# Another order of the first steps in a fused mLSTM and feed-forward kernel

## The chip, the cores and the metric

The kernel runs on one core of a Trainium2 chip. The metric is the device time of one execution in microseconds (us), as the median of several runs. Of TensorE (PE in the profile, PEld for its weight loads), VectorE (DVE), ScalarE (ACT), GpSimd (POOL) and SyncE (SP), the last one here only issues transfers.

## The reference

An mLSTM cell runs over 768 steps for 4 batches of 8 heads with 40 numbers each. Its output, as 3072 rows of 320 numbers, goes through a multiplicative feed-forward network.

```python
for t in range(S):
    m_new = np.maximum(f_gate[:, :, t] + m, i_gate[:, :, t])
    f_stab = np.exp(f_gate[:, :, t] + m - m_new)
    i_stab = np.exp(i_gate[:, :, t] - m_new)
    m = m_new
    C = f_stab[:, :, None, None] * C + i_stab[:, :, None, None] * np.einsum('bhd,bhe->bhde', vt, kt)
    n = f_stab[:, :, None] * n + i_stab[:, :, None] * kt
    h_tilde = np.einsum('bhde,bhe->bhd', C, qt)
    nq = np.einsum('bhd,bhd->bh', n, qt)[:, :, None]
    denom = np.maximum(np.abs(nq), 1.0)
    o = 1.0 / (1.0 + np.exp(-o_gate[:, :, t]))
    y[:, :, t] = o * h_tilde / denom
...
a = x @ w1          # x: (3072, 320), w1 and w2: (320, 1024)
b = x @ w2
h = a * b @ w3      # (1024, 1024)
return (h @ w_out)  # (1024, 320)
```

All data are float32. The weights come as 64-bit numbers, two 32-bit words each, and the kernel turns them into float32 on the chip.

## The kernel before, in words

**Units.** The sequence is cut into chunks of 128 steps (two halves of 64). A unit is one chunk of one batch with all 8 heads: 24 units, numbered from 0, the four batches of chunk 0 first. For a unit, PE transposes k and q (`turn`, tiles `pt`, copied to `kT` and `qT` by ACT), makes the scores inside each half (`cell<-qT,kT`) and the two updates of the state (`cell<-vw,kbuf`). POOL makes the weighted values `vw` (`weighted`, line 326). Decay weights `pw` come from a DVE transpose of a small table (`rows_of_u`, L291), an exponential on ACT (`weights`, L299, eight pieces) and a triangular mask on POOL (`masks`, L304). DVE multiplies scores by them (L388). In the next step PE makes the unit's output from these products (`ph` for units 0 and 1, `cell<-vbuf,pw` later) and from the state (`cell<-state,qT`); DVE scales and sums it (L412 to L419), forms the denominator (L427 to L430), and multiplies by the output gate (L432, L434) to `y`. `out_gate` is the tanh for it on ACT (L266). The state is updated by a DVE copy or addition (L397, L395), a POOL multiplication (`decayed`, L331) and a DVE addition (L403).

**Steps.** The loop over `s` handles unit s's scores and unit s−1's output in `quarter_work`. From step 2 on it also holds feed-forward work. A block is 128x512 products of w1 (`pa`) and of w2 (`pb`) for 256 rows; `up` does 256 of the 320 rows of the contraction, `up_rest` the remaining 64 against the tile `wr`. ACT then copies `pa` (`a_sb`, L624) and DVE multiplies it with `pb` (L625). Steps 2 to 5 have one block each, all on the rows of units 0 and 1; steps 2 and 3 use the first half of the weights' columns, steps 4 and 5 the second half. `x_trans` (tiles `px`, `xT`) turns a unit's `y` into the feed-forward input; `twice` (POOL, L465) doubles 64 of its columns first. `warm` issues fill matmuls.

**Words.** `fetch` (L180) loads a set of weight words. `scale_next` takes the next set through two ACT operations (L187, L191); for the first two sets DVE does the second (L189). `convert` makes float32 of it in two DVE operations (L195, L196). The sets of the first half are w1 twice, w2 twice and `wr`; the same five follow for the second half, then others.

**Order.** All transfers except the input gate and the output are issued from SP in program order. The order on each engine is that of the program, with a few operations held behind a named one (`issue_after`, `keep_order`); PE's order is chained by hand (`in_order`). So the change, which moves calls, moves instructions. Four PSUM buffers (`mps`) go round among the transposes and blocks: an operation that takes one waits until the reader of the fourth before it is done.

In step 2 the function `between` runs after unit 1's output and before unit 2's scores: it holds `x_trans` of units 0 and 1, conversions, the turn of unit 2 and the first block.

Of the kernel before, what the change touches and what calls it, by code (L numbers as in the profile page):

```python
# [16 lines left out]
def kernel(  # L17
# [211 lines left out]
    def scale_next(early=False):  # L229
        scaled.append(pend.pop(0))  # L230
        scale(scaled[-1][1], early)
# [101 lines left out]

    def quarter_work(s, rest, between):

# [53 lines left out]
        with tc.issue_after(first_read.ins) if first_read else nullcontext():  # L389
            if den:  # L390
                den()
            if n < NU:

                if c:
                    nc.vector.tensor_tensor(out=second, in0=pc[:, 0], in1=second, op=OP.add)  # L395
                else:
                    nc.vector.tensor_copy(out=second, in_=pc[:, 0])  # L397
                if len(ends) > 1:
                    decayed(after, second, n, 1)
            if den:  # L400
                den()
            if n < NU and len(ends) > 1:
                nc.vector.tensor_tensor(out=after, in0=pc[:, 1], in1=after, op=OP.add)  # L403
            if den:
                done = den()
        return done if den else first_read

    def outputs(n, pi, ph):
# [181 lines left out]
    for x in range(2):  # L590
        mm(pd[halves[x]], odd[:, x].to_broadcast([RG, L]), pick.rearrange("p j g c -> p (j g c)"))
    cols_of_u()
    nc.scalar.copy(out=decay.rearrange("p j c -> p (j c)"), in_=pd)
    rows_of_u(1)
    nc.scalar.activation(out=g, in_=U, func=AF.Exp)
    scale_next(True)
    convert()
# [142 lines left out]
    todo = w12[5:] + [("wo", i, 0) for i in range(FO)] + [("w3", ko, part) for ko in range(FO) for part in range(2)]  # L740
    n_cvt = [0, 0, 2, 0, 1, 2, 3, 3, 3] + [2] * 6
    n_fetch = [5, 5, 10]
    pinned, ahead = 32, 9
# [3 lines left out]
    for s in range(len(n_up)):  # L747
# [4 lines left out]
        if s < 3:  # L752
            if s == 2:
                for _ in range(3):
                    fetch(*todo.pop(0))
            load(s + 2, slice(0, 2))
            if s == 1:
                load_o(2)
            if s == 2:
                for _ in range(2):  # L760
                    fetch(*todo.pop(0))
                fetched = 10
            load(s + 2, slice(2, 3))
            if s:
                load_o(s + 2)
        elif s + 2 < NU:
            load(s + 2)
            load_o(s + 2)
# [26 lines left out]
        open_ups = [up(*x) for x in now] if s != 2 else []  # L795
        if s == 3:
            turn(3)
        def rest():
            for x in open_ups:
                up_rest(*x)  # L800
            if seven:
                seven[2]()
            if s == 3:
                for _ in range(2):
                    convert()

        def between():
            twice(1)
            weighted(2)
            rows_of_u(3)  # L810
            for _ in range(3):
                scale_next()
            for n in range(2):
                x_trans(n)
                if n == 0:
                    warm(5)
            for _ in range(3):
                convert()
            turn(2)
            block = up(*now[0])  # L820
            weighted(3)
            weights(3)
            masks(3)
            out_gate(2)
            convert()
            up_rest(*block)

        gated = None
        if s <= NU:
            gated = quarter_work(s, rest, between if s == 2 else None)  # L830
        else:
            rest()
        with tc.issue_after(gated.ins) if gated else nullcontext():
            if seven:
                seven[3]()
            if NY <= s - 2 < NU:
                x_turn(s - 2)
            for n in () if s == 1 else (s + 2,) if s < B else (s + 2, s + 3) if s == B else (s + 3,):
                if n < N_U:
                    rows_of_u(n)  # L840
            if N_DVE <= s + 1 < NU:
                gated = turn(s + 1)
            if s - 2 in range(4 * GT - 1, NU, GT):
                token_sums((s - 2) // GT)
        if s == 0:
            weighted(1)
            weights(1)
            masks(1)
            gate_cols(g, gT, nc.scalar.copy)
        if s == NU:  # L850
            cell_psum.close()
            banks.extend([ps_m] * 3 + [ctx.enter_context(tc.tile_pool(name="ps_x", bufs=4, space=bass.MemoryType.PSUM))] * 4)
        if s in (2, 3):
            turned, converted = 2, converted + (4 if s == 2 else 2)
        if s + 1 < N_DVE:
            if s not in (1, 2):
                turn(s + 1)
            while turned < min(s - 1, NY):
                x_trans(turned)
                turned += 1  # L860
        if s < NU:
            if 0 < s < NU - 1 and s != 2:
                if s != 1:
                    weighted(s + 1)
                weights(s + 1)
                masks(s + 1)
            if s != 2:
                out_gate(s)
# [50 lines left out]
```

## Time and profile before

| what | value |
|---|---|
| median of 3 runs | 436.58 us (435.71 to 437.52) |
| profiled execution | 436.73 us |
| its span | 435.0 us |
| mean granted clock of TensorE | 0.984 |
| PE busy | 421.6 us |
| DVE busy | 306.3 us |
| ACT busy | 151.8 us |
| POOL busy | 92.8 us |
| transfers | 51.14 MB, mean 118 GB/s |

The span is the time from the first to the last instruction of the program that the profiler saw; the execution's own time has 1.73 us more around it. Busy time is the sum of an engine's instructions, where a matmul that stands in the pipeline counts as busy. "Clock" is the share of TensorE's full clock that it was granted. A wait is told as the engine and line that waited, then who ended it: the time in total, how often, and the longest.

In the timeline a row is: start, duration, engine, line, operation, out<-in, shape, count, and in brackets the engine's idle time before it and who ended that.

### The profile page before, as it was taken

The page shows a single profiled execution, that of the slowest core. Times are in us where ns is not written, and L with a number is a line of the kernel's source. Part 1 is how long each engine was busy: PE and PEld are TensorE (multiplying, and loading weights), DVE is VectorE, ACT ScalarE, POOL GpSimd, SP SyncE. Part 2 cuts the span into 40 slices and gives each one's busy share as a digit, 9 for nine tenths or more (in the row PEclk, how much of TensorE's full clock was granted, in tenths as well). Part 3 has the DMA queues.
Part 4 walks back from the last instruction along what each step waited for, and adds up shares of the span by engine and source line. Part 5 has one row for each costly group of instructions (what it writes and reads, how often), then busy time and mean ns, then how long its engine had stood idle before and what let it go on. Part 6 is the DMA issues. An engine that isn't in the chain of part 4 may idle for free.

```text
span 435.0 us, 12730 instructions
## 1 busy us (share of the span) xinstructions
PE 421.6 (97%) x5233; PEld 335.1 (77%) x5233; DVE 306.3 (70%) x633; ACT 151.8 (35%) x409; POOL 92.8 (21%) x163
## 2 busy tenths in 40 slices
PE   7699899999999999999999999999999999999996
PEld 6688778878788787887777778788777777777774
DVE  6756886778949778777746968698998876444800
ACT  4866563566724523530332203123211111110110
POOL 4530342333303203303317623022100000000000
PEclk9979799999999999999999999999999999999999
DMA  8999977498987776884426676746221110000001
GB/s 186 213 183 232 222 111 131 126 198 169 205 197 134 171 174 141 173 168 92 102 63 135 151 130 145 160 98 137 53 54 37 35 35 15 17 17 15 2 30 46
DMA packets 135211, 51.14 MB, mean 118 GB/s; under 512 B 109360, under 2 KB 126960, under 8 KB 135152
## 3 DMA queue, kind: packets, MB, share of 16 engines
q1 hardware_dynamic: 131552, 46.29, 51.7%
q10 hardware_dynamic: 3600, 4.03, 2.7%
q8 instruction: 41, 0.67, 0.7%
q14 instruction: 18, 0.15, 0.1%
HBM read 44.50 MB, written 5.80 MB: 116 GB/s over the span
## 4 chain that ended last, share of the span: by engine, by line
PE 71%; SPq 8%; issue 8%; DMA 5%; POOL 3%; DVE 2%; ACT 1%; POOLq 0%; DVEq 0%; ACTq 0%
PE cell L92 19%; PE pa L92 19%; PE pb L92 12%; PE po L92 10%; PE wp L92 6%; PE p L92 5%; SPq L135 4%; DMA raw<-in_moe_w_dram 3%; SPq L180 2%; POOL pw L304 1%; POOL raw L645 1%; SPq L149 1%; SPq L144 1%; DVE w3T L652 1%; PE pt L95 1%
## 5 line engine op out<-in xcount | busy, mean ns | idle before, releaser
L92 PE MATMUL po<-w3o,ab 128*128 128x320 f32 x256 | 70.6, 433 | 0.0
L92 PEld LDWEIGHTS po<-w3o,ab 128*128 128x128 f32 x256 | 48.4, 190 | 19.7 <-issue 0.4
L92 PE MATMUL pa<-xT,w 128*128 128x256 f32 x240 | 61.5, 387 | 1.6 <-ACT xT L475 1.6
L331 POOL TENSOR_TENSOR state<-state,decay 128x164 f32<-128x164 f32 x40 | 19.7, 493 | 168.9 <-DVE state L395 139.2
L92 PEld LDWEIGHTS pa<-xT,w 128*128 128x128 f32 x240 | 45.3, 194 | 9.5 <-ACT xT L475 2.1
L299 ACT ACTIVATE pw<-pw,aT 128x64 f32<-128x64 f32 x184 | 46.4, 339 | 3.3 <-ACT o_sb L727 1.9
L304 POOL TENSOR_SCALAR_AFFINE_SELECT pw<-pw 64x512 f32<-64x512 f32 x48 | 38.2, 796 | 37.0 <-ACT pw L299 24.7
L92 PE MATMUL pb<-xT,w 128*128 128x256 f32 x192 | 45.4, 379 | 0.0
L92 PEld LDWEIGHTS pb<-xT,w 128*128 128x128 f32 x192 | 36.5, 190 | 5.0
L92 PE MATMUL pa<-xT,wr 64*64 64x256 f32 x384 | 37.0, 386 | 0.5 <-DVE wr L196 0.5
L92 PE MATMUL pb<-xT,wr 64*64 64x256 f32 x384 | 36.4, 380 | 0.0
L92 PE MATMUL wp<-wo,w3T 128*128 128x320 f32 x128 | 35.9, 433 | 0.2
L624 ACT ACTIVATE a_sb<-pa 128x512 f32<-128x512 f32 x24 | 14.3, 596 | 61.5 <-PE pb L92 61.5
L92 PE MATMUL cell<-w3o,ab 128*128 128x320 f32 x128 | 35.4, 432 | 0.0
L625 DVE TENSOR_TENSOR ab<-pb,a_sb 128x512 f32<-128x512 f32 x24 | 16.4, 686 | 25.8 <-ACT a_sb L624 25.7
L727 ACT COPY o_sb<-po 128x320 f32<-128x320 f32 x16 | 6.8, 426 | 74.4 <-PE po L92 74.4
L92 PEld LDWEIGHTS cell<-w3o,ab 128*128 128x128 f32 x128 | 24.3, 190 | 9.5
L672 DVE SCALAR_TENSOR_TENSOR a_sb<-pa,wo 128x512 f32<-128x512 f32 x12 | 8.3, 690 | 32.6 <-PE pa L92 32.6
L92 PEld LDWEIGHTS wp<-wo,w3T 128*128 128x128 f32 x128 | 23.8, 190 | 9.6 <-DVE ab L625 0.4
L92 PEld LDWEIGHTS pa<-xT,wr 64*64 64x64 f32 x384 | 18.9, 132 | 15.4 <-issue 8.8
L419 DVE TENSOR_TENSOR h<-cell,h 64x164 f32<-64x164 f32 x88 | 28.7, 326 | 1.7
L92 PEld LDWEIGHTS pb<-xT,wr 64*64 64x64 f32 x384 | 20.1, 133 | 3.0
(141 smaller groups left out, 730.4 us busy)
## 6 DMA issues: line engine op xcount, KB each, us to landing
raw<-in_moe_w_dram SPq DMA_DIRECT2D x64, 128.0 KB, 3.2
kbuf<-in_k_dram SPq DMA_DIRECT2D x24, 160.0 KB, 4.2
vbuf<-in_v_dram SPq DMA_DIRECT2D x24, 160.0 KB, 4.7
o_in<-in_o_gate_dram SPq DMA_DIRECT2D x24, 160.0 KB, 4.8
out_dram<-o_sb ACTq DMA_DIRECT2D x24, 160.0 KB, 1.8
pw<-U_d SPq DMA_DIRECT2D x28, 128.0 KB, 3.6
raw<-in_moe_w_dram SPq DMA_DIRECT2D x5, 512.0 KB, 6.8
raw<-in_moe_w_out_dram SPq DMA_DIRECT2D x8, 320.0 KB, 3.8
```

Source lines behind the costliest of these rows:

```text
L92: in_order(nc.tensor.matmul(out, lhsT=lhsT, rhs=rhs, start=start, stop=stop))
L95: in_order(nc.tensor.transpose(out, in_, ident[0:n, 0:n]))
L135: nc.sync.dma_start(out=dst, in_=rows(src, n))
L180: nc.sync.dma_start(out=dst, in_=src)
L299: nc.scalar.activation(out=pw[:, h, :], in_=src[:, h, :], func=AF.Exp, bias=aT[:, c, b * H + h:b * H + h + 1])
L304: nc.gpsimd.affine_select(out=pw[r], in_=pw[r], compare_op=OP.is_ge, fill=0.0, base=0, pattern=[[0, H], [1, L]], channel_multiplier=-1)
L331: nc.gpsimd.tensor_tensor(out=new, in0=old, op=OP.mult, in1=decay[:, b * NP:(b + 1) * NP, 2 * c + x:2 * c + x + 1] .to_broadcast([P, NP, D1]))
L419: nc.vector.tensor_tensor(out=part, in0=ph[x][halves[e]], in1=part, op=OP.add)
L624: nc.scalar.mul(out=a_sb, in_=pa, mul=UP ** -2)
L625: nc.vector.tensor_tensor(out=ab_t[gr][j][:, fs[0]:fs[-1] + 1, t0:t0 + a_sb.shape[-1]], in0=pb, in1=a_sb, op=OP.mult)
L672: nc.vector.scalar_tensor_tensor(out=out, in0=p, scalar=UP ** -2, in1=q, op0=OP.mult, op1=OP.add)
L727: nc.scalar.copy(out=o_sb, in_=po)
```

## The change

Nothing is added to or taken from the computation but one fill matmul; calls are put at other places.

- Before the loop: the scaling of the second set goes ahead of the copy of `decay` and the exponential of `g` on ACT; its DVE part ahead of `rows_of_u(1)`.
- Step 0: `rows_of_u(2)` is no longer called there; POOL has the masks of unit 1 ahead of its weighted values.
- Step 1: two sets (the third and fourth) are scaled at its end; the weights and masks of unit 2 are no longer made there.
- Transfers: step 1 fetches the first two second-half sets ahead of unit 3's k and q and the third between them and v; step 2 fetches the last two ahead of unit 4's k and q. The output gates of units 2 and 3 are loaded later.
- Step 2: `between` has the block's `up` ahead of `turn(2)`, `rows_of_u(2)` and `rows_of_u(3)` between conversions, one fill matmul fewer, and the second state update of unit 1, which is put off to here; the weights, masks and weighted values of unit 3 go behind `quarter_work`, and three conversions to the end of the step.
- Steps 3, 4 and 5: the turn of unit s follows the block's `up`; at steps 3 and 4 the output gate of the unit before is taken inside. In step 3 the last two conversions of the second half go from ahead of unit 2's output to `late`, behind unit 3's masked scores.

```diff
-    def quarter_work(s, rest, between):
+    def quarter_work(s, rest, between, late):
...
-                if len(ends) > 1:
+                if n == 1:
+                    put_off.append((after, second, pc))
+                elif len(ends) > 1:
                     decayed(after, second, n, 1)
+            if late:
+                late()
             if den:
                 den()
-            if n < NU and len(ends) > 1:
+            if 1 != n < NU and len(ends) > 1:
                 nc.vector.tensor_tensor(out=after, in0=pc[:, 1], in1=after, op=OP.add)
...
     cols_of_u()
+    scale_next(True)
+    rows_of_u(1)
     nc.scalar.copy(out=decay.rearrange("p j c -> p (j c)"), in_=pd)
-    rows_of_u(1)
     nc.scalar.activation(out=g, in_=U, func=AF.Exp)
-    scale_next(True)
     convert()
...
-    n_cvt = [0, 0, 2, 0, 1, 2, 3, 3, 3] + [2] * 6
-    n_fetch = [5, 5, 10]
+    n_cvt = [0, 0, 3, 0, 1, 2, 3, 3, 3] + [2] * 6
+    n_fetch = [0, 0, 10]
...
-            if s == 2:
-                for _ in range(3):
-                    fetch(*todo.pop(0))
+            for _ in range((0, 2, 2)[s]):
+                fetch(*todo.pop(0))
             load(s + 2, slice(0, 2))
             if s == 1:
-                load_o(2)
+                fetch(*todo.pop(0))
             if s == 2:
-                for _ in range(2):
-                    fetch(*todo.pop(0))
+                load_o(3)
                 fetched = 10
             load(s + 2, slice(2, 3))
             if s:
-                load_o(s + 2)
+                load_o(2 * s)
...
-        if s == 3:
-            turn(3)
+        if s in (3, 4, 5):
+            turn(s)
         def rest():
             for x in open_ups:
                 up_rest(*x)
             if seven:
                 seven[2]()
-            if s == 3:
-                for _ in range(2):
-                    convert()
+            if s in (3, 4):
+                out_gate(s - 1)
 
         def between():
             twice(1)
+            x_trans(0)
+            warm(4)
+            x_trans(1)
+            scale_next()
+            convert()
+            convert()
+            rows_of_u(2)
+            convert()
+            rows_of_u(3)
+            weights(2)
+            after, second, pc = put_off.pop()
+            decayed(after, second, 1, 1)
+            nc.vector.tensor_tensor(out=after, in0=pc[:, 1], in1=after, op=OP.add)
             weighted(2)
-            rows_of_u(3)
-            for _ in range(3):
-                scale_next()
-            for n in range(2):
-                x_trans(n)
-                if n == 0:
-                    warm(5)
-            for _ in range(3):
-                convert()
+            masks(2)
+            block = up(*now[0])
             turn(2)
-            block = up(*now[0])
-            weighted(3)
-            weights(3)
-            masks(3)
-            out_gate(2)
+            up_rest(*block)
+            scale_next()
+
+        def late():
             convert()
-            up_rest(*block)
+            convert()
...
-            for n in () if s == 1 else (s + 2,) if s < B else (s + 2, s + 3) if s == B else (s + 3,):
+            for n in () if s < 2 else (s + 2,) if s < B else (s + 2, s + 3) if s == B else (s + 3,):
...
         if s == 0:
-            weighted(1)
             weights(1)
             masks(1)
+            weighted(1)
...
-            turned, converted = 2, converted + (4 if s == 2 else 2)
+            turned, converted = 2, converted + (3 if s == 2 else 2)
         if s + 1 < N_DVE:
-            if s not in (1, 2):
+            if s not in (1, 2, 3, 4):
                 turn(s + 1)
...
-            if 0 < s < NU - 1 and s != 2:
-                if s != 1:
+            if s == 1:
+                scale_next()
+                scale_next()
+            if 1 < s < NU - 1:
+                if s != 2:
                     weighted(s + 1)
                 weights(s + 1)
                 masks(s + 1)
-            if s != 2:
+                if s == 2:
+                    weighted(3)
+            if s not in (2, 3):
                 out_gate(s)
```

## The prediction, before the changed kernel was timed

> **What bounds the kernel now.** I read the page first, then TensorE's waits, then stretches of the span with the granted clock, then the timeline of the two stretches where TensorE stands.
>
> ```profile
> PE 421.6 (97%) x5233; PEld 335.1 (77%) x5233; DVE 306.3 (70%) x633; ACT 151.8 (35%) x409; POOL 92.8 (21%) x163
> ...
> PE ph L92 <- DVE pw L388: 2.3, 2, 1.2
> PE px L95 <- DVE y L434: 1.2, 1, 1.2
> PE cell L92 <- issue: 1.5, 1, 1.5
> PE pa L92 <- DVE wr L196: 0.5, 1, 0.5
> ```
>
> TensorE (PE) is busy for 97%: 13.4 us of idle time in 435.0, of which 9.0 lie before 65 us and 3.3 in the last 35 (from 120 to 400 us it is busy 279.8 of 280). So a gain is to be had at the front alone, and it lasts to the end if PE is ahead when it leaves the front. The stretches (busy us of PE, PEld, DVE, ACT, POOL, then clock, DMA share, GB/s) show the second thing:
>
> ```profile
> 17.25:20.67 3.42, 2.29 (x114) 2.05 (x102) 2.81 (x9) 2.64 (x10) 2.09 (x5) 1.00 1.11 237
> 20.67:24.08 3.41, 2.21 (x11) 2.21 (x12) 3.10 (x9) 3.30 (x7) 0.96 (x2) 0.50 1.19 131
> 24.08:27.49 3.41, 3.41 (x17) 3.32 (x17) 3.14 (x6) 2.03 (x5) 1.09 (x2) 0.50 0.94 150
> ...
> 44.56:47.97 3.41, 1.37 (x27) 0.69 (x29) 3.30 (x11) 3.41 (x12) 0.00 (x0) 1.00 1.05 176
> 47.97:51.39 3.42, 3.42 (x129) 3.34 (x126) 2.92 (x7) 0.13 (x1) 3.14 (x5) 0.50 1.02 365
> 51.39:54.80 3.41, 3.41 (x14) 3.23 (x15) 3.17 (x11) 2.02 (x5) 0.48 (x3) 0.50 0.99 144
> ```
>
> Twice, after a stretch in which PE was busy for only 2.29 or 1.37 us, it gets half its clock for 6.83 us. And why it stood before 47.97:
>
> ```profile
> 43.15 0.68 ACT L187 ACTIVATE raw<-raw 128x512 f32<-128x512 f32 x1 [1.67 <-DMA raw<-in_moe_w_dram]
> 43.86 0.43 DVE L195 TENSOR_SCALAR wr<-raw 128x512 uint32<-128x512 uint32 x1 [1.65 <-ACT raw L187]
> ...
> 45.04 0.49 DVE L412 TENSOR_TENSOR h<-cell,gT 128x328 f32<-128x328 f32 x1
> 45.18 0.43 PE L92 MATMUL pa<-xT,wr 64*64 64x256 f32 x1 [0.49 <-DVE wr L196]
> ...
> 47.03 0.69 DVE L388 TENSOR_TENSOR pw<-cell,pw 128x512 f32<-128x512 f32 x1
> ...
> 47.82 1.00 PE L92 MATMUL cell<-vbuf,pw 64*64 64x41 f32 x32 [1.54 <-issue]
> ...
> 58.72 0.63 PE L92 MATMUL cell<-vbuf,pw 64*64 64x41 f32 x32
> ```
>
> The last words of the second half (wr) land at 43.07; DVE stands 1.65 us for them, and the outputs of unit 2 (L412) and the masking of unit 3's scores (L388), long ready, are queued behind. PE loses 0.49 us for wr and 1.54 us for L388, then works at half clock. I use 58.72, the first matmul of unit 4's outputs, as my milestone.
>
> [...] both slow stretches are 6.83 us, two windows, and unit 3's cell matmuls took 3.56 us (47.82 to 51.38) against 1.85 for a unit at full clock. [...] landings of 160 KB row tiles (rows of 40 numbers) follow each other by 0.75 to 1.3 us, those of 512 KB of words by 1.5 to 2.4.
>
> **The change, part by part.** I wrote the four engines' queues in both orders and carried start times forward with durations of this trace. The old order so treated meets the trace within about 0.5 us.
>
> *Up to 21 us.* DVE's L189 moves ahead of unit 1's rows, into 1.66 us of idle DVE time (its words landed at 11.34). Then L388 of unit 0 starts when its mask is done, about 14.0 instead of 14.68; PE's ph at 14.7 (15.41). On POOL the mask of unit 1 goes ahead of its weighted values (0.74 us): the values are ready at 17.4, so PE's state products wait some 0.6 us, but rows 2 (0.70) leave DVE and L403's wait (0.54) is put off, so ph of unit 1 starts at 18.1 (19.05) and y(0) is done at 19.8 (21.73). ACT's weights(2), 2.0 us, move behind the words: y(1) at 22.5 (24.44).
>
> *First block ahead of the turn.* PE: px(1) 22.9, its copy, pa at 24.3 (27.02). I keep the early half clock: the idle time from 17.25 to 24.08 is 2.2 us, before 2.3. So pa takes 3.3 us instead of 1.73, pb 27.6 to 29.3, the turn 0.9, the wr part 0.87 to 31.05, scores and states 1.0: the next block starts at 32.05 against 32.75. Gain **0.7**; most of the lead is eaten at half clock. The put-off state update of unit 1 (POOL 0.46, DVE 0.33), one fill matmul fewer, the moved rows and output gates (0.47 each on ACT) I cost at nothing: DVE is idle from 27.5 to 31.9, and the state is read only at unit 5. Without that cover they cost their own durations, 2 us in all.
>
> *SP's queue.* The issues are moved, none added. With each tile at its own spacing, the five sets of second-half words land at 28.1, 30.2, 33.8, 37.2, 40.1 (before 32.70, 35.09, 36.56, 40.21, 43.07). Paid by unit 3's k, q, v (31.2, 32.2, 34.7, needed at 35.5, 35.9 and 36.3) and unit 4's k, q (41.0, 42.0, needed at 45): hidden, with 3 us or more for all but v, which has 1.6. If 3 us late they would stop PE by as much.
>
> *Unit 3.* PE: pa, pb, turn, wr part to 37.25, outputs of unit 2 to 38.2. ACT: a_sb at 31.25 (0.5), a pair of scalings (1.13), weights(3) 1.92, two pairs 2.26, kT and qT 0.96, ready at 38.15, just in time. Next block's pa at 39.2; before, 41.07 less the turn (0.93) that now comes later is 40.14. Gain **0.94**.
>
> *The new wait.* `late` puts the conversions of the last two sets behind L388 of unit 3 on DVE. From a_sb's end at 38.65: ab 0.6, L412 0.54, four adds 1.37, den and L388 0.7, den and L397 0.35, L195+L196 1.25: 43.5. PE's pb wants that set at 41.15 and stands **2.4** us; queued behind it are the turn, the rest, all of unit 3's outputs. Against the 0.49 of before that is 1.9 lost. The wr set is converted at 44.65, in time for 45.95. Then L388 (done at 42.0) keeps nobody waiting: **1.54** removed. Milestone at full clock: 45.95 + 0.87 + 1.9 (cells) + 0.3 (px) + 3.46 + 0.88 + 0.87 = 54.2.
>
> *Sum at the milestone.* 58.72 − 54.2 = 4.5: early 0.94, idle −1.9 + 1.54, half clock removed 3.75 (46.28 to 58.72 holds 7.15 us of work and 1.54 of idle), 0.2 rounding. From it goes what the new gap costs: 2.4 us of idle is more than the 2.04 that halved the clock before. A window of 3.41 us at half does half its work, 1.65 or so. The first window after it would hold pb, transposes and wr matmuls, full work as in 24.08 to 27.49, after which the clock came back: one window. 4.5 − 1.65 = **2.9** us. Behind the milestone the order is the same, PE's wait for xT (0.84) stays, and I let the lead stand. The profiled execution takes 436.73 with a span of 435.0, 1.73 around it: 432.1 + 1.73 = 433.8, which is 0.15 above the median (436.58), so **433.7**.
>
> **Rivals.** My forecast, one late half-clock window: 433.7, chance 0.38.
> - None: the gap is split between two windows (13.84 to 17.25 us held 1.15 us of idle time and the clock stayed). 436.6 − 4.5 = 432.1, chance 0.22.
> - Two, as before: 436.6 − 1.2 = 435.4, chance 0.20. For it: that is what both stretches of the trace show.
> - Slower: PE's new gaps (1.0 and 0.8 us about px(1), then 2.4) are counted harder, and the half clock lasts a window or two longer at both places. Gain = 4.5 − 1.65 n for n half windows besides the two early ones; from n = 3 it is a loss, and n = 4 gives 438.7. Against it: full tiles run after both gaps. Chance 0.12.
> - It doesn't carry: DVE reaches unit 4's product at 55.5, 0.5 after PE's release, where before it idled 0.83; if DVE or the transfers bound the steps after 60 us, the time stays at 436.4. Chance 0.08.
>
> **How the numbers follow.** A measurement of this kernel tells about 0.5% (2.2 us) from no change. Faster: the first two, less the part of the first above 434.4: 0.56. Same 0.33, slower 0.11. The range, from none (with 0.7 us of error in my sums) to no gain: 431.4 to 436.6; it leaves out the slower case and little else.
>
> **What would show it.** Right: words landing near 28, 30, 34, 37, 40; pa of the third block near 32; a PE wait for DVE's w (L196) of some 2.4 us near 41 to 44; no wait at L388 of unit 3; the milestone near 55.8 and one half window before it. Wrong: k or v of unit 3 waited for by PE or POOL, a half clock through pa and pb past 28 us, or PE idle time after 65 us grown by what the front gained.

## The result, and the profile after

The changed kernel takes 438.19 us (median of 20 runs, 435.68 to 442.1), the kernel before 436.63 beside it (20 runs, 434.62 to 438.49): a ratio of 1.0036, 95% interval 1.0015 to 1.0058. It is slower by 1.6 us where 2.9 us of gain was forecast, and lies above the forecast range. The profiled execution took 437.39 us with a span of 435.6 and a mean granted clock of 0.988. The ratios of the experiments below leave out runs more than 1.5% above the fastest of their kernel (three in e2, one in e3, two in e8), the medians keep them, and a ratio is not the plain quotient of two medians.

From the page after, engines and the queue that carries instructions (packets, MB, share):

```profile
PE 420.2 (96%) x5231; PEld 332.8 (76%) x5231; DVE 308.2 (71%) x633; ACT 151.8 (35%) x409; POOL 94.4 (22%) x163
...
q8 instruction: 41, 0.67, 0.7%
```

TensorE has the same work. Its waits after:

```profile
PE pb L92 <- DVE w L196: 2.4, 1, 2.4
PE pa L92 <- ACT xT L481: 2.2, 3, 0.8
...
PE cell L92 <- issue: 1.5, 2, 0.8
PE ph L92 <- DVE pw L388: 1.4, 2, 0.9
PE cell L92 <- POOL vw L326: 0.9, 1, 0.9
...
PE px L95 <- DVE y L440: 0.4, 1, 0.4
```

The wait of 2.4 us at pb was forecast, to the digit. L388 of unit 3 keeps nobody waiting any more. What was not forecast: 1.5 us at "issue" in the middle of cell groups, and xT, which is now waited for three times instead of twice: the 0.57 us at the first block is new. In the kernel before that line was:

```profile
PE pa L92 <- ACT xT L475: 1.6, 2, 0.8
```

The stretches with their clock (columns as before: PE, PEld, DVE, ACT, POOL, clock, DMA share, GB/s):

```profile
16.37:19.79 3.42, 1.60 (x80) 1.34 (x74) 2.28 (x7) 2.46 (x5) 1.31 (x2) 1.00 1.11 254
19.79:23.20 3.41, 2.76 (x60) 2.54 (x57) 1.31 (x3) 0.81 (x2) 0.24 (x1) 0.50 0.85 101
23.20:26.61 3.41, 2.97 (x14) 2.35 (x12) 3.10 (x9) 0.48 (x1) 0.87 (x2) 0.50 0.85 204
...
43.68:47.09 3.41, 1.18 (x5) 1.06 (x6) 3.14 (x8) 1.14 (x5) 2.35 (x3) 1.00 0.98 150
47.09:50.51 3.42, 3.42 (x22) 2.52 (x24) 2.81 (x6) 1.17 (x2) 1.96 (x4) 0.50 1.11 278
50.51:53.92 3.41, 3.41 (x143) 3.12 (x138) 2.10 (x6) 1.52 (x4) 0.00 (x0) 1.00 1.22 265
```

In this trace and in that of the kernel before the clock changes only at points that lie whole multiples of 3.41 us apart: it is half from 19.79 to 26.61 and from 47.09 to 50.51 here, from 20.67 to 27.49 and from 47.97 to 54.80 before, with 20.48 us, six times 3.41, of full clock between the two stretches in either. Such a piece of 3.41 us is called a window here. What it does to TensorE's work: in the kernel before, one group of four transposes starts 0.86 us after the other at half clock (25.31 and 26.17) and 0.44 us at full (36.30 and 36.74). The cell matmuls of a unit, 3.56 us there at half clock, take 2.03 at full from first start to last end (38.18 to 40.21), not the 1.85 of the prediction.

One late half-clock window instead of two, after the stall at pb: as forecast. In the front there are two in this execution, as before. Yet unit 4's output, forecast at 55.8, begins at 58.49. Two timelines tell where it went. First up to the first block, rows of three engines:

```profile
17.03 0.73 POOL L326 TENSOR_TENSOR vw<-vbuf,wT 128x328 f32<-128x328 f32 x1
...
17.82 0.68 PE L92 MATMUL cell<-vw,kbuf 64*64 64x41 f32 x32 [0.94 <-POOL vw L326]
...
18.63 0.69 DVE L388 TENSOR_TENSOR pw<-cell,pw 128x512 f32<-128x512 f32 x1 [0.84 <-PE cell L92]
...
19.38 1.52 PE L92 MATMUL ph<-vbuf,pw 64*64 64x41 f32 x30 [0.88 <-DVE pw L388]
...
22.08 0.75 PE L92 MATMUL cell<-state,qT 40*64 40x41 f32 x17 [0.65 <-issue]
...
25.82 0.88 PE L95 MATMUL px<-ident,y 128*128 128x128 f32 x3 [0.44 <-DVE y L440]
...
27.26 1.99 PE L92 MATMUL pa<-xT,w 128*128 128x256 f32 x8 [0.57 <-ACT xT L481]
```

In brackets stands what each row waited for: POOL's vw, behind the mask, holds the state products; these hold DVE's L388, which the forecast had let start without them; it holds ph. Then comes an idle of 0.65 us that no engine explains, and the first block begins at 27.26, not 24.3. Second, the late stall:

```profile
41.67 0.69 ACT L187 ACTIVATE raw<-raw 128x512 f32<-128x512 f32 x1
...
42.23 0.68 ACT L191 ACTIVATE raw<-raw 128x512 uint32<-128x512 uint32 x1
...
42.95 0.59 PE L92 MATMUL pb<-xT,w 128*128 128x256 f32 x2
...
43.66 0.69 DVE L388 TENSOR_TENSOR pw<-cell,pw 128x512 f32<-128x512 f32 x1
...
44.58 0.41 DVE L195 TENSOR_SCALAR w<-raw 128x512 uint32<-128x512 uint32 x1
45.13 0.73 DVE L196 CUSTOM_DVE_ANT_0 w<-raw,w 128x1024 uint16<-128x1024 uint16 x1
...
45.91 1.81 PE L92 MATMUL pb<-xT,w 128*128 128x256 f32 x6 [2.37 <-DVE w L196]
```

pb's words were scaled before 41.8 (the two ACT rows shown are those of the set after). DVE had them ready to convert and made unit 2's output and unit 3's masked scores first: L195 begins at 44.58, pb stands until 45.91.

The time of a run is best read in three stretches: from the start to unit 2's output (the first `cell<-vbuf,pw` matmul), from there to unit 4's output, and to the end of the span. These are my subtractions from the timelines of three executions of each kernel (the first of each, and e13 to e16 below), in us:

| execution | to unit 2's output | to unit 4's output | to the end |
|---|---|---|---|
| before | 38.18 | 20.53 | 376.29 |
| before, e13 | 37.28 | 19.65 | 376.42 |
| before, e14 | 38.60 | 19.68 | 377.99 |
| after | 39.16 | 19.32 | 377.16 |
| after, e15 | 41.38 | 19.38 | 376.05 |
| after, e16 | 42.42 | 19.31 | 376.07 |

On the mean the first stretch is 3.0 us longer, the second 0.6 shorter, the third 0.5 shorter: together 1.9 us slower, the medians say 1.6.

Four executions of the experiments keep one of the two fronts, up to unit 2's output: e5 that of the kernel before (39.88), e2, e6 and e11 that of the changed kernel (40.63, 40.23, 40.57). With them the first stretch is 37.3 to 39.9 us (38.5 on the mean) against 39.2 to 42.4 (40.7): the change made it some 2.2 us longer, and the two ranges overlap a little. The half-clock windows in it are 2, 1, 1 and 3 in the kernel before, and 2, 3, 4, 3, 3 and 2 in the changed kernel.

### The profile page after: what moved, and what is told of

Same layout as the page of the kernel before. It is cut to its first block, busy times and chain, and to the rows that moved or that the text cites. A ratio compares the mean times of both kernels' runs of the same rounds, so it can differ in the third digit from the quotient of the medians.

```text
span 435.6 us, 12724 instructions
## 1 busy us (share of the span) xinstructions
PE 420.2 (96%) x5231; PEld 332.8 (76%) x5231; DVE 308.2 (71%) x633; ACT 151.8 (35%) x409; POOL 94.4 (22%) x163
## 4 chain that ended last, share of the span: by engine, by line
PE 78%; issue 8%; POOL 4%; DVE 4%; ACT 3%; DMA 2%; SPq 1%; DVEq 0%; POOLq 0%; ACTq 0%
PE pa L92 20%; PE cell L92 20%; PE pb L92 13%; PE po L92 10%; PE wp L92 6%; PE p L92 5%; PE pt L95 2%; POOL pw L304 1%; POOL raw L651 1%; DMA raw<-in_moe_w_dram 1%; DVE w3T L658 1%; PE px L95 1%; ACT pw L299 1%; DMA kbuf<-in_k_dram 1%; POOL vw L326 1%
## 5 line engine op out<-in xcount | busy, mean ns | idle before, releaser
L92 PEld LDWEIGHTS pa<-xT,w 128*128 128x128 f32 x240 | 44.5, 190 | 10.1 <-ACT xT L481 3.0
L304 POOL TENSOR_SCALAR_AFFINE_SELECT pw<-pw 64x512 f32<-64x512 f32 x48 | 38.7, 807 | 41.4 <-ACT pw L299 39.9
L92 PEld LDWEIGHTS cell<-w3o,ab 128*128 128x128 f32 x128 | 24.3, 190 | 9.5
```

Of the source, the lines that this page charges most:

```text
L92: in_order(nc.tensor.matmul(out, lhsT=lhsT, rhs=rhs, start=start, stop=stop))
L304: nc.gpsimd.affine_select(out=pw[r], in_=pw[r], compare_op=OP.is_ge, fill=0.0, base=0, pattern=[[0, H], [1, L]], channel_multiplier=-1)
```

## The experiments

Every median is compared with runs of the kernel before on the same chip; its own median there is 436.3 to 436.6 us (e1 to e12). The three stretches, where they are given, come from the one profiled execution of each kernel.

### e1, e2, e3: values first, no `late`, both

e1 puts unit 1's weighted values first on POOL:

```diff
         if s == 0:
+            weighted(1)
             weights(1)
             masks(1)
-            weighted(1)
```

> The changed kernel with unit 1's weighted values ahead of its mask on POOL again. Theory of the queues: the masking of unit 1's scores on DVE also waits for the state products, which wait for these values; it starts near 17.8 us instead of 18.63, unit 1's output is 0.8 us or more earlier, and the time falls by 1 to 1.5 us, to about 437. Theory of the transfers (the earlier words crowd the rows and PE's own instructions): no change, 438.2.

Measured 439.2 us (436.88 to 440.89, 10 runs; before 436.58), ratio 1.0051 (1.0027 to 1.0074). No gain: the expectation failed. But this execution holds a clean measurement. It has the stall of pb and no half clock after it:

```profile
48.54:51.96 3.42, 1.50 (x7) 1.30 (x8) 3.15 (x7) 0.83 (x4) 2.61 (x4) 1.00 0.39 107
51.96:55.37 3.41, 3.41 (x141) 2.99 (x139) 3.20 (x8) 2.03 (x4) 1.70 (x3) 1.00 0.79 215
```

and its second stretch is 17.70 us where the changed kernel's is 19.32: from the pa ahead of the stall to unit 4's output 15.74 us against 17.37. The late half-clock window costs 1.63 us, as forecast (1.65).

e2 takes `late` away: the two conversions stand ahead of unit 2's output again.

```diff
+            if s == 3:
+                late()
...
-            gated = quarter_work(s, rest, between if s == 2 else None, late if s == 3 else None)
+            gated = quarter_work(s, rest, between if s == 2 else None, None)
```

> The changed kernel with the last two conversions of step 3 ahead of unit 2's output again, as before the change. Theory of the queues: the PE wait of 2.37 us for DVE's w goes, at most 0.5 us comes back at unit 3's outputs, no late half-clock window; the milestone (unit 4's outputs) moves from 58.49 to about 55.5 and the time falls by 2.5 to 3 us, to about 435.3. Theory of the transfers: under 0.5 us.

Measured 435.69 us (432.72 to 441.35, 22 runs), ratio 0.9963 (0.9945 to 0.9981): as expected, 2.5 us below the changed kernel. The second stretch fell to 17.06 us, and the first stayed long (40.63). So `late` costs 2.5 us here.

e3 is both edits.

> Both of the two edits before. Theory of the queues: the two gains add up, about 434.2 us, faster than the kernel before. Theory of the transfers: no change, 438.

Measured 434.95 us (432.31 to 440.44, 12 runs), ratio 0.9946 (0.9918 to 0.9973). Second stretch 17.06 again, first 37.75. It is faster than the kernel before, but its first stretch is one of a wide scatter: e1's, with the same order on POOL, was 43.72. Some 1.9 us of that lie ahead of the edit: in e1's execution unit 0's scores began at 13.55 us (11.4 to 12.3 in e2, e3, e5, e6, e11 and the executions of the table), and four transposes ahead of them took 1.06 us, as they did at half clock in the kernel before (the group at 26.17 us), instead of 0.60.

### e4: the old transfers in the changed kernel

```diff
-    n_fetch = [0, 0, 10]
+    n_fetch = [5, 5, 10]
...
         if s < 3:
-            for _ in range((0, 2, 2)[s]):
-                fetch(*todo.pop(0))
+            if s == 2:
+                for _ in range(3):
+                    fetch(*todo.pop(0))
```

(and the places of the output gates and of the last two sets in SP's order as before)

> The changed kernel with the transfers in the order of before (second-half words behind unit 3's rows, output gates at their old places). Theory of the queues: the DVE queue sets when the words are converted, with the last set landing near 43 and its turn on DVE at 45.8, so the time stays within 0.5 us of 438.2. Theory of the transfers: 1 to 1.5 us faster, as before the change, about 436.7. If the earlier words were what the new order lives on: 2 to 3 us slower.

Measured 438.73 us (434.95 to 441.38, 22 runs), ratio 1.0040 (1.0017 to 1.0062); second stretch 19.39 us, with the same 2.37 us at pb. The earlier words bring nothing while `late` decides when they are converted.

### e5: `late` alone, in the kernel before

```diff
+            if late:
+                late()
             if den:
                 den()
             if n < NU and len(ends) > 1:
...
-            if s == 3:
-                for _ in range(2):
-                    convert()
...
+        def late():
+            convert()
+            convert()
```

> The kernel before, with only its two conversions of step 3 moved into `late`. By the theory that the price of `late` is the wait of pb for words that stand behind unit 2's output on DVE, less the wait for L388 that the move takes away: pb waits about 2.4 us and the 1.54 us wait for L388 goes, so about 437.4 us. By the rival that `late` costs its 2.5 us wherever it is put: 439.1.

Measured 435.62 us (432.93 to 439.4, 22 runs; before 436.31), ratio 0.9981 (0.9960 to 1.0001). Both expectations were too high: in the kernel before, `late` costs nothing and may gain. TensorE's timeline ahead of its pb:

```profile
41.83 0.66 PE L95 MATMUL pt<-ident,kbuf 128*128 128x128 f32 x4
42.32 0.60 PE L95 MATMUL pt<-ident,q_all 128*128 128x128 f32 x4
42.76 1.89 PE L92 MATMUL pa<-xT,w 128*128 128x256 f32 x8
44.49 0.59 PE L92 MATMUL pb<-xT,w 128*128 128x256 f32 x2
45.58 1.56 PE L92 MATMUL pb<-xT,w 128*128 128x256 f32 x6 [0.50 <-DVE w L196]
```

The turn of unit 4 (pt) stands ahead of the block here and fills 0.9 us in which DVE works towards the words. pb waits 0.50 us, no half clock follows, and the second stretch takes 16.00 us against 19.65 to 20.53. In the changed kernel the turn stands behind the block: TensorE arrives earlier, by the turn's 0.9 us, at pb, and waits there for the same DVE.

### e6 and e10: the stall filled with matmuls

```diff
         for p, wt in ((pa, w1), (pb, w2)):
+            for _ in range(fills if p is pb else 0):
+                mm(pb[:, 0, :], ident, x[:, 0, cs])
...
-        open_ups = [up(*x) for x in now] if s != 2 else []
+        open_ups = [up(*x, fills=9 if s == 4 else 0) for x in now] if s != 2 else []
```

> The changed kernel with nine more matmuls of the identity on the tokens (256 columns each, into pb's own bank, overwritten after) between pa and pb of step 4, so that PE works while it waits for the late words. They add work (some 2 us) and no result. By the theory that part of the loss is the half clock that the idle 2.4 us bring: about 436.9 us, a higher mean clock and no half-clock window near 47 to 51 us. By the rival that the wait alone is the loss: 438.2, or slightly more if the fill outlasts the wait.

Measured 442.19 us (439.02 to 442.65, 6 runs; before 436.31), ratio 1.0104 (1.0063 to 1.0145). The late half clock is gone, the second stretch is 19.27 us: the nine fills took 3.9 us where 2.4 were to be filled, and what the clock gained they took. But the third stretch, far behind the fills, takes 381.31 us, 4.2 more than in the changed kernel. A row of TensorE's timeline there, and the line of its waits:

```profile
101.24 0.31 PE L92 MATMUL cell<-vw,kbuf 64*64 64x41 f32 x4 [1.60 <-issue]
```

```profile
PE cell L92 <- issue: 4.3, 3, 1.8
```

Three such idles (1.60, 1.76 and 0.92 us, at 101, 151 and 199 us) stand in the middle of cell groups whose operands are long there. I counted TensorE's records in order of start (matmuls, weight loads and 94 of its sequencer, 10,556 in the changed kernel). The three idles begin at record 3265, 4545 and 5825; those of the changed kernel (22.08 and 61.22 us) at 705 and 1985. Every one is 193 plus a multiple of 256 (to within a record). 10,556 records hold 41 such borders from 193 on, and the instruction queue shown above moved 41 packets, 0.67 MB, 16 KB each. In the changed kernel the packets that precede the two idles land at 20.52 and 59.80 us, 1.4 to 1.6 us before TensorE goes on. That one packet brings TensorE 256 instructions is my estimate from these counts.

e10 is e6 with 256 more records in all, so that the borders fall at the same matmuls as in the changed kernel:

```diff
-    warm(8)
+    warm(4, 59)
```

(the second argument adds matmuls of 32x32 weights on 8 columns)

> e6_filled_stall once more, with four of the warming matmuls at the start replaced by 59 very short ones, so that all of PE's instructions but these stand 256 records later than in the changed kernel and the borders of 256 fall at the same matmuls as there. By the theory that the 4.3 us that e6_filled_stall lost at 101, 151 and 199 us were waits for instructions, made by its 36 more records: these three are gone, and what is left is the filled stall without its half clock, about 436.9 us (438.2 if the half clock costs nothing). By the rival that the fill itself brought them: still 441 to 442.

Measured 440.84 us (439.9 to 442.04, 6 runs; before 436.5), ratio 1.0097 (1.0074 to 1.0120). The time was not the forecast one, because the short matmuls took far longer than I had counted: the warming ended at 10.1 us instead of 5.4, and unit 0's scores began at 17.30 instead of 11.46, since the work in between took as long as at half clock too (four transposes 1.06 us). But the three idles are gone. TensorE's longest waits are now:

```profile
PE pa L92 <- ACT xT L483: 2.2, 3, 0.8
PE fill L92 <- POOL ident masks.py:199: 1.6, 1, 1.6
PE px L95 <- DVE y L442: 1.4, 1, 1.4
PE ph L92 <- DVE pw L390: 1.1, 1, 1.1
```

with no "issue" among them. So it is the 36 records that the fills added, not the fills' work, that cost the 4 to 5 us there (381.31 against 376.09 here, and 377.16 in the changed kernel). These are one execution each; an idle at a given border comes and goes from execution to execution (e15 and e16 below).

### e9: the borders moved in the changed kernel

```diff
-    warm(8)
+    warm(6, 34)
```

> The changed kernel with two of the eight warming matmuls at the start replaced by 34 very short ones (32x32 weights, 8 columns), which have no result and lie beside the gates' work on DVE: 128 more records of PE ahead of everything. The idle of 0.65 us at 22.08 and of 0.83 us at 61.22, for which the profile names no other engine, begin at the 705th and the 1985th record of PE, and the 16 KB packets that carry PE's own instructions land some 1.5 us before. By the theory that PE waits there for its next 256 instructions, the two waits move with the count of instructions or go: no idle at the same two matmuls, about 437.2 us (436.7 if neither comes back elsewhere). By the rival that these matmuls wait for something of their own (a semaphore that the profile doesn't show), both stay where they are in the work: 438.2.

Measured 441.4 us (439.77 to 445.1, 6 runs), ratio 1.0125 (1.0087 to 1.0163). The time tells nothing of the idles, for the same reason as in e10 (unit 0's scores at 15.48 us). The places do: an idle of 1.35 us again begins at record 705, which is now a matmul of `cell<-vw,kbuf` and no longer of `cell<-state,qT`; none is at 1985 and a new one of 0.44 us is at 6337 = 193 + 24 x 256. They go with the count, not with the work.

### e7 and e8: two parts of the change, without `late`

e7 is e2 with the turn of unit 2 ahead of the first block:

```diff
-            block = up(*now[0])
             turn(2)
+            block = up(*now[0])
```

> The changed kernel without `late` (as e2_no_late), and in step 2 the turn of unit 2's k and q again ahead of the first block. By the prediction's step 2 the block's place is worth 0.7 us: about 436.4 us. By the rival that PE has the same work in front of the same wait in either order: 435.7, as e2_no_late.

Measured 434.85 us (432.94 to 437.7, 22 runs; before 436.31), ratio 0.9957 (0.9939 to 0.9975): the same as e2 (0.9963) or a little better. The gain of 0.7 us isn't there. In e7's timeline the turn runs while ACT copies xT, and pa starts behind it without a wait; what the block's new place costs is measured at full clock under e13 to e16.

e8 is e2 with e4's transfers.

> The changed kernel without `late`, and with SP's transfers in the order of the kernel before. By the theory that the earlier words pay only where the conversions stand ahead of L388: the conversions wait for words again as they did before (1.65 us), L388 of unit 3 is late by some 1.5 us, about 437.2 us. By the rival that the order of the transfers is worth nothing in either place: 435.7, as e2_no_late.

Measured 436.95 us (434.05 to 441.38, 14 runs), ratio 0.9994 (0.9969 to 1.0019). Its second stretch is 19.39 us against 17.06 in e2, with 1.50 us of TensorE at L388 again. Here the earlier transfers are worth 1.3 us in the median (the two intervals overlap) and 2.3 in the stretch; in e4 they were worth nothing.

### e11: the turn ahead of the block, with `late`

```diff
-        if s in (3, 4, 5):
-            turn(s)
+        if s == 3:
+            turn(3)
...
-            if s not in (1, 2, 3, 4):
+            if s not in (1, 2):
                 turn(s + 1)
```

> The changed kernel with `late`, but with the turns of k and q of steps 4 and 5 again ahead of those steps' blocks, as before the change. By the theory that neither `late` nor the moved turn costs anything alone, and that the 2.37 us of pb come from both (the turn's 0.9 us of transposes stood between unit 3's products and the block and covered the conversion; in e5_late_alone pb waited 0.50): pb waits about 1.4 us less than 2.37, about 436.7 us. By the rival that DVE's late end at the output sets the time whatever PE does ahead of pb: 438.2.

Measured 436.53 us (435.04 to 439.42, 14 runs; before 436.5), ratio 1.0000 (0.9977 to 1.0024): 1.7 us better than the changed kernel, as expected. pb waits 0.64 us and no half clock follows; the second stretch is 17.26 us, of which 0.68 are a wait of the turn for unit 4's k. The loss at pb is that of two edits together.

### e12: e3 and e7 together

> e3_both (no `late`, values ahead of the mask) with the turn ahead of the block in step 2, as in e7_turn_first. If the three edits are independent of one another: 434.95 less 0 to 0.8, so 434.2 to 435. It leaves of the change the earlier transfers, the masks' order and the turns of steps 4 and 5 behind their blocks; if it is faster than the kernel before by 0.5%, these are what is good in the change. By the rival that e3_both and e7_turn_first were drawn low: 435.7.

Measured 435.39 us (432.17 to 437.39, 22 runs; before 436.5), ratio 0.9970 (0.9954 to 0.9985). Faster than both kernels, but not better than e3 or e7, and between the two expectations: the edits of the front don't add up.

### e13 to e16: each kernel again

> The kernel before, unchanged, for a second profiled execution. In the first, unit 2's output began at 38.18 us, and from there to unit 4's output it took 20.53 us, with a half clock from 47.97 to 54.80; unit 4's output to the end took 376.29. By the theory that the 3.75 us of half clock that the prediction took off belonged to that one execution and not to the kernel: another execution has the half clock elsewhere, the first stretch is 1 to 3 us longer, the second that much shorter, and the end is again 434.5 to 436. By the rival that the kernel before always loses them there: 20 to 20.5 us in the second stretch again.

> As e13_before_again, a third execution of the kernel before: the same two expectations. Whether the stretch up to unit 2's output is 38 us in all of them tells whether the changed kernel's 39.16 us is a loss of the change.

> The changed kernel, unchanged, for a second profiled execution. In the first, unit 2's output began at 39.16 us, from there to unit 4's output 19.32, to the end 377.16. By the theory that the wait of pb and the waits for instructions belong to the kernel: the second stretch is again 19 to 19.5 us with 2.4 us of wait at pb, and the third 377.0 to 377.5 with an idle at the 1985th record of PE. By the rival that these two were chance: 17 to 18 and 376.1. The first stretch differs by 1 to 4 us from execution to execution by either.

> As e15_after_again, a third execution of the changed kernel: second stretch 19 to 19.5 us and third 377.0 to 377.5 if both losses belong to the kernel; the first stretch says whether it is always behind the kernel before (38.2 in its first execution) or varies about it.

One run each: 435.06 and 437.98 us (before), 438.53 and 439.51 (after); the stretches stand in the table above. Of the kernel before, both have less late half clock than the first execution (one window and none, not two), and yet the second stretch is only 0.9 us shorter: neither of the two expectations held. Of the changed kernel, the stall of pb came back both times (2.37 and 2.35 us), the idle at record 1985 did not; that one came in e14, the kernel before (1.12 us). The first stretch of the changed kernel is longer in all three. In e16, around its first block:

```profile
19.07:22.49 3.42, 2.36 (x47) 2.21 (x47) 1.93 (x6) 1.58 (x3) 0.24 (x1) 0.50 1.17 131
22.49:25.90 3.41, 2.69 (x27) 2.61 (x28) 1.66 (x6) 0.48 (x1) 0.00 (x0) 0.50 0.83 203
25.90:29.31 3.41, 2.39 (x8) 1.61 (x8) 3.31 (x6) 1.44 (x3) 2.20 (x3) 0.50 1.09 253
29.31:32.73 3.42, 3.42 (x9) 2.70 (x9) 2.76 (x6) 2.21 (x9) 0.36 (x1) 0.50 0.99 236
```

Four half-clock windows, one after the other, and the block lies in the last two: its pa took 3.78 us (28.40 to 32.18), as it did in e15 with 3.61, where 1.89 is full clock. The kernel before, in e13, from px of unit 1 to its block:

```profile
25.03 0.54 PE L95 MATMUL px<-ident,y 128*128 128x128 f32 x3
25.41 0.60 PE L95 MATMUL pt<-ident,kbuf 128*128 128x128 f32 x4
25.84 0.60 PE L95 MATMUL pt<-ident,q_all 128*128 128x128 f32 x4
26.28 1.89 PE L92 MATMUL pa<-xT,w 128*128 128x256 f32 x8
...
31.84 1.99 PE L92 MATMUL pa<-xT,w 128*128 128x256 f32 x8
```

The fills last until y is there, the turn until ACT's copy of xT is: TensorE hardly stands (0.09 us ahead of px), and the clock is back. After the change it stands at both places (0.44 and 0.57 us). The same way at full clock with the block first, in e3:

```profile
24.61 0.67 PE L95 MATMUL px<-ident,y 128*128 128x128 f32 x3 [0.45 <-DVE y L440]
25.85 1.99 PE L92 MATMUL pa<-xT,w 128*128 128x256 f32 x8 [0.57 <-ACT xT L481]
...
32.31 1.99 PE L92 MATMUL pa<-xT,w 128*128 128x256 f32 x8
```

From px to the first block it takes 1.24 us here and 1.25 in e13: the block begins no earlier without the turn ahead of it, because it waits for ACT's copy. From px to the second block it takes 7.70 us here and in e4, e8 and e11, which have the block first too and the clock full; with the turn first it takes 6.81 (e13) and 6.76 (e14), and 7.27 and 7.42 where another wait stands in it (e5, 0.44 us for wr; e12, 0.32 for qT). So the block's new place costs up to the turn's own 0.9 us.

## Why the prediction was wrong, step by step

- **Up to 21 us: this step failed, and with it the way to px of unit 1.** It let L388 of unit 1 start by its scores alone, so that the late vw cost PE 0.6 us and ph came at 18.1. L388 waited for the state products too (0.84 us, for those begun at 17.82), and ph came at 19.38, 19.70 and 19.66 in the three executions. From there to the end of unit 1's outputs TensorE took 3.45, 3.73 and 4.30 us instead of the 1.60 of the trace that I read. Of this 0.65, 1.61 and 1.19 us are the idle at record 705, which no step had; the kernel before had it in e13 and e14 (0.95 and 2.21), and not in that trace. The rest, 0.5 to 1.5 us, goes with the half clock, which now fell on these outputs, while the forecast left it at its old place behind them. So px of unit 1, put at 22.9, came at 25.82, 26.42 and 26.96: 3.5 us late on the mean.
- **First block ahead of the turn: failed.** The gain of 0.7 us was not there. Taken from the block, the turn no longer covers xT (0.57 us), and at full clock the new place costs up to 0.9 us. The length of this step was met all the same, by luck: from px of unit 1 to the second block the forecast had 9.15 us with its half clock, and the executions took 7.90, 9.52 and 10.03, for the half clock ran on over the block in two of them. The kernel before took 8.07, 6.81 and 6.76.

  What in the change makes the way to px longer, and adds the half clock, the runs don't settle. With the values first the way from unit 1's scores to px of unit 1 took 8.3 to 8.4 us (e1, e3, e12) against 9.6 to 10.0 in the changed kernel's three executions, but without that edit it took 7.9 to 9.8 in e2, e4, e6, e7, e8 and e11, and e1 was not faster for it. No edit that takes back a part of the front (e1, e3, e12 the values, e7 and e12 the turn, e4 and e8 the transfers) surely shortens it, and the scalings and conversions that were moved there were not tried one by one. That the half clock comes from the new waits, and not from chance, is likewise only read from six executions against four.
- **SP's queue: right.** The five sets landed at 28.69, 30.23, 33.96, 38.60 and 40.67 (28.1, 30.2, 33.8, 37.2, 40.1 forecast; the fourth is 1.4 us late), unit 3's k, q, v at 31.02, 32.26 and 34.72 (31.2, 32.2, 34.7). What they are worth depends on who comes next: nothing behind `late` (e4), 1.3 us without it (e8 against e2).
- **Unit 3: failed with the front**, whose lead it carried on. Its own part, from the second block to that of step 4, took 7.4 us in all three executions where the sum had 7.15.
- **The new wait: right in mechanism and size** (2.4 us forecast, 2.37, 2.37 and 2.35 measured). But the forecast charged all of it to `late`, and e5 and e11 show that the turn moved behind the block is the other half: with the turn in its old place 0.50 and 0.64 us are left. From pa to unit 4's output at full clock it took 15.74 us (e1) against 15.0 in the sum: 0.5 of it because DVE's words came later after pa, 0.3 in the steps behind.
- **The late half-clock window: right**, one window, 1.63 us.
- **The half clock removed, 3.75 us: a number of one execution, and too large for it.** Two windows at half clock, 6.83 us, can cost half of that, 3.41; so the 7.15 us of work that the sum subtracts are some 0.3 too few, about what the steps behind pb took beyond it. And the kernel's second stretch took 19.65 and 19.68 us in two other executions with one late window and with none. Its half clock mostly takes the place of a wait: in that stretch TensorE stood idle for 2.04, 2.35 and 3.45 us with two windows, one and none. The mean clock of a run tells how many windows it had (its missing share, times two, times the span, over 3.41 us: 0.012 x 2 x 435.6 / 3.41 = 3.1 for the three of the changed kernel's profiled execution; one at the very end of the span counts too). A straight line through all 139 timed runs of the kernel before that stand beside e1 to e12 rises by 0.37 us for each window, one through the changed kernel's 20 runs by 1.28; and the changed kernel has 3.8 windows on the mean where the kernel before has 2.7. This term belongs to the comparison with the kernel before; the forecast time itself comes from the steps above.
- **Behind the milestone: right.** 376.3 us forecast, 377.16, 376.05 and 376.07 measured; 0.83 us of the first of these is the idle at record 1985.

The rivals: the fourth came nearest, "PE's new gaps are counted harder", with 438.7 us, and it was given 0.12. It had the place right (about px of unit 1) and the effect (half clock through the block in two executions of three). Its number is luck: it stands for four half windows besides the two early ones, and the three executions had one, two and three, for which its rule gives a gain of 2.85, a gain of 1.2 and a loss of 0.45 us. The lateness ahead of px was not in it. Against it stood that full tiles run after both gaps; yet the block's pa ran at half clock in e15 and in e16, there through two windows.

Why it was wrong, in one sum of the executions' means: 3.7 us in the front (3.5 of them ahead of px of unit 1, 0.2 in unit 3's part), 0.75 between pa of step 4 and unit 4's output, 0.1 behind, together 4.6 us between the forecast span of 432.1 and the measured mean of 436.7.

## What to carry to other kernels

A piece of work that is moved away from in front of a wait was the cover of that wait: ask of every moved piece which engine's late result it used to hide, at the old place as well as what it hides at the new one; here 0.9 us of transposes hid two such waits, and an edit that was harmless alone (`late`) cost 2.5 us with it. Before taking off the price of a slow clock or of an idle, look at a second execution: such windows fall elsewhere each time (late in the span two, one and none in three executions of the kernel before), and behind another bound they cost little (0.37 us each over its 139 runs). When an engine of many short instructions stands in the middle of a group for no reason that the profile names, count its instructions (here such idles lay whole multiples of 256 records apart).

## What the runs showed of the hardware

- TensorE's waits for instructions, as I read them from e6, e9 and e10: 0.35 to 2.4 us at borders of 256 records, most of them in cell groups (matmuls of 64x41, some 14 ns apart; a unit's 128 cell matmuls are, with their weight loads, 256 records in 1.96 us, from 38.18 to 40.14 in the kernel before). All 18 executions together have 29 idles of over 0.25 us at such borders, and each ends 1.25 to 1.61 us after the landing of one 16 KB packet, the one that was sent after the border before. In the first execution of the kernel before, that packet landed at 18.76 us, record 705 came at 20.2, and TensorE did not wait. Where a border falls is moved by any edit ahead of it: 36 records more cost 4 to 5 us over the next 140 us (e6, one execution). When a packet is asked for is not settled: those of the 29 idles began 0.4 to 4.6 us after the border before.
- The busy share of a window doesn't decide the clock by itself. With 1.18 us of full tiles (the changed kernel) the next window was at half. With 1.50 us of full tiles it was at full clock in e1, and at half in e10, where 0.67 of them were transposes. With 1.76 and 1.78 us, nearly all of small matmuls, it was at half in e13 and at full in e14.
- A short matmul is not a cheap one in the warming: 59 of 32x32 weights on 8 columns, in place of four full ones, took 4.7 us more (8.47 against 3.78).
